# Chunked attention into a Fourier mixing layer: values of the first batch by two queues, column sines late, mirrored halves for the second batch, and instruction orders from fixed lists

## The chip, the cores and the metric

The kernel runs on one core of a Trainium2 chip. The metric is the device time of one execution in microseconds. Engines are named as in the profile: PE (matmul) and its weight loads PEld, DVE (vector), ACT (scalar), POOL (GpSimd) and SP (which here only issues DMAs). DMAs are issued by SP, by ACT and by POOL, each on a queue of its own.

## The reference

Four batches, eight heads, 768 positions, head width 64. The first part is attention in chunks of 32 queries, each of which sees its own chunk, 16 keys to the left, 8 to the right and 8 memory keys:

```
for c in range(nc):
    k_full = concat([mem_k, k[c_start - 16 : c_end + 8]])
    v_full = concat([mem_v, v[c_start - 16 : c_end + 8]])
    a = softmax(q_c @ k_full.T / 8)
    out[c] = a @ v_full
```

The heads are joined to rows x of 768 x 512 per batch, and a mixing layer follows:

```
X = fft(x, axis=1);  X = fft(X, axis=2);  mixed = real(X)
u = x + mixed
un = (u - mean(u)) / sqrt(var(u) + 1e-6)
out = u + relu(un @ w_ch1) @ w_ch2        # 512 -> 2048 -> 512
```

## The kernel before, in words

**Attention.** Work goes by pairs of heads: 16 pairs, n = 0 to 15, four per batch. For a pair, POOL issues the loads of q and k (`e_load_qk`, L375 for the first three batches), SP issues the values (`e_load_v`, seven DMAs: L388 once, L384 four times, L393 twice) into one of four value tiles `va`, PE turns q and k (L403), ACT or DVE copies them out (`e_qT` L421, `e_kT` L446), PE makes scores (L459), ACT the exponentials (L469, L494), PE the values (`e_values`, L511, tiles `xa` and `xo` for the two halves), and DVE normalizes (L521, L522). The value tiles have edges that `e_edges` (L345 to L347) zeroes on DVE or POOL before the load may write.

**Fourier step.** The transform over positions and columns is done by matmuls with cosine and sine tables, which the kernel makes itself at the start: `e_iota` writes index ramps on POOL, DVE turns them to angles (`rS`, `yS` for the rows, `rD`, `yD` in the tile `tri` for the columns), and ACT takes sines (`e_sines`, L1201). `e_negatives` and `e_table_rows` on POOL make the negated tables. The first batch has its own finer-grained path (`first_fourier`: folds, hi and lo parts in half precision, row matmuls at L717, joins at L731), the later ones go through `fourier` (row matmuls L583). Column matmuls come in two forms: `e_columns` (L756, eight matmuls of 256 columns per tile of 128 rows) and, from batch HALVED on, `h_columns` (L777), which uses the mirror symmetry of the column tables and leaves the combination to ACT (`h_copy`, `h_ends`), DVE (`h_mix`, `h_sum`, tile `mix`) and POOL (`h_sum_back`, L817).

**MLP.** Each batch has three thirds j of 256 rows. Layer 1 is `e_ch1` (L894, tile `ph`) with the ReLU on ACT (L903). Layer 2 is either plain (`e_ch2`, L912, added at L919) or, for the thirds in FAST, a scheme of seven products of half-size blocks (`e_prod`, L961) with sums on DVE (`e_s`, L949; results added at L966). A third in FAST takes normalized rows with their scale; the others are scaled at the end by `rstd`. MIXED is the batch in which both forms occur.

**Order.** The kernel does not leave the order to chance. Every piece of work is a task: engine, cost, prerequisites, the buffers that it takes and gives. `Plan.order` plays them through with a model of engine and DMA times and emits the instructions in that order; each engine then runs its own in sequence. Before, tasks have ranks, at each step an engine takes the first by rank that is ready in the model, and a table `moved` overrides about eighty of the ranks. `settled` sets these ranks and calls `order`. Where PE would be idle at the start, filler matmuls on a zero tile (`idle`, L1025 and L1033) stand in the order. `t_gate`, a tiny copy on POOL (L1093) that reads the last value tile of batch 0, keeps POOL's later loads (batch 1 and the weights, `weights`, L1229 and L1234) behind the first batch's values.

Of the kernel before, what the change touches and what calls it, by code (L numbers as in the profile page):

```python
# [10 lines left out]
FP32 = mybir.dt.float32  # L11
# [6 lines left out]
LEFT = 16  # L18
RIGHT = 8
# [18 lines left out]
class Plan:  # L38
# [20 lines left out]
    def add(self, engine, cost, emit, after=(), take=(), give=(), rank=None, moved=0.0,  # L59
            loose=False, late=0.0, filler=False, behind=None, lag=0.0, pick=None, grain=0.1, head=1.0, dense=0.15, mode=""):  # L60
# [3 lines left out]
                 late=late, filler=filler, behind=behind, lag=lag, picks=[pick] if pick else [], grain=grain, head=head, dense=dense, mode=mode)  # L64
        self.tasks.append(t)
        return t

    def share(self, now):
# [4 lines left out]
        while any(left.values()):  # L73
            heads = [xs_[0] + [xs_[0][0]["grain"], q] for q, xs_ in left.items() if xs_]
            live = [h for h in heads if h[2] <= at + 1e-9]
            whole = sum(h[3] for h in live)
            slow = {q: 0.94 if len(live) > 1 and xs_ and xs_[0][0]["grain"] < 0.05 else 1.0
                    for q, xs_ in left.items()}
            step = min([h[1] * whole / h[3] / slow[h[4]] for h in live]
# [5 lines left out]
            for q, xs_ in left.items():  # L85
                if xs_ and xs_[0][2] <= at - step + 1e-9:
                    xs_[0][1] -= step * slow[q] * xs_[0][0]["grain"] / whole
# [14 lines left out]
    def settled(self, moved):  # L102

        for no, rank in moved.items():
            self.tasks[no]["rank"] = rank
        return self.order()

    def order(self):
# [9 lines left out]
        while any(waiting.values()):  # L118
# [5 lines left out]
            for e, ts_ in waiting.items():  # L124
                if idle.get(e, 0.0) > now or (e == "SP" and self.clear > now):
                    continue
                held = False
                for t in ts_:
                    slack = (self.SLACK if e == "PE" and now > self.FIRST and not t["filler"]
                             else 0.0)  # L130
                    if held and not t["loose"]:
                        continue
                    if any(a["done"] is None
                           or (a["end"] > now if a["engine"] == e else a["done"] > now - slack - t["lag"])
                           for a in t["after"]):
                        held = held or (e == "SP" and not t["loose"])
                        continue
# [11 lines left out]
                    if any(self.free[tag] < m for tag, m in need.items()):  # L149
                        held = held or (e == "SP" and not t["loose"])  # L150
                        continue
# [34 lines left out]
            if not moved:  # L186
                recent = [t for t in recent if t["done"] + 8.0 > now] + placed[known:]
# [3 lines left out]
                         + [t["done"] + x for t in recent for x in (0.0, self.SLACK, 4.0, 8.0)  # L191
# [9 lines left out]
def kernel(  # L201
# [15 lines left out]
    P = 128  # L217
# [11 lines left out]
    HALVED = 2  # L229
# [41 lines left out]
    FAST = [(1, 1), (1, 2)] + [(b, j) for b in range(2, B) for j in range(3)]  # L271
    MIXED = 1
# [17 lines left out]
    tri = fpool.tile([P, 3, 2, HD], FP32, tag="hT", bufs=1, name="tri")  # L290
# [87 lines left out]
    def e_load_v(n):  # L378
# [3 lines left out]
        def run(p0, count, t0, nt, key, hh):  # L382
            vb = v[b, 2 * pr + hh]
            nc.sync.dma_start(v1[p0:p0 + count, hh, t0:t0 + nt, 0:D],  # L384
                              bass.AP(tensor=vb.tensor, offset=vb.offset + key * D,
                                      ap=[[D, count], [64 * D, nt], [1, D]]))

        nc.sync.dma_start(v1[OWN:OWN + 64, :, 0, 0:D],  # L388
                          v[b, 2 * pr:2 * pr + 2, 0:64].rearrange("h p d -> p h d"))
# [602 lines left out]
    t_mkf = add("ACT", 1.3, e_mkf, moved=2.04, grain=0.077)  # L992
# [19 lines left out]
    t_kzs = add("ACT", 2.9, e_kzs, [t_table], rank=-2)  # L1012
    for i in range(NV):
# [57 lines left out]
    t_gate, LATE, t_flip = None, 0.3, [None]  # L1071
# [4 lines left out]
    def attention(n):  # L1076
# [5 lines left out]
                      take=(("qs", "ks")[i],), moved=2.02 if b >= TURNED else 1.2, grain=0.089 if b >= TURNED else 0.081,  # L1082
# [3 lines left out]
        lv = add("SP", 2.5, lambda: e_load_v(n), [t_edges[n] if n < NV else None, t_used.get(("va", n % NV))],  # L1086
                 behind=t_x2.get(b - 2),
# [516 lines left out]
```

## Time and profile before

| what | value |
| --- | --- |
| time, median of 3 runs | 274.52 us (274.36 to 275.14) |
| the profiled execution, time | 274.5 us |
| the profiled execution, span | 272.8 us |
| PE busy | 264.2 us, 97% |
| DVE busy | 196.8 us, 72% |
| ACT busy | 160.6 us, 59% |
| POOL busy | 83.3 us, 31% |
| mean DMA rate | 147 GB/s |
| granted PE clock | 1.00 |

The span reaches from the first to the last instruction. Busy times are shares of that span. PE's busy time includes the filler matmuls at the start (11.0 us at L1025 and 7.2 us at L1033, counted as the profile counts them). A wait of an engine is named by what ended it.

### The profile page before, as it was taken

Reading aid. Unit: us, or ns where it says so; the run is one execution under the profiler, and the core shown is the slowest. Engines: PE = TensorE matmul, PEld = TensorE weight load, DVE = VectorE, ACT = ScalarE, POOL = GpSimd, SP = SyncE. Lnnn points to the kernel's source line nnn. Section 1 sums busy time; section 2 is a strip of 40 time slices with the busy share of each in tenths; the row PEclk is TensorE's granted clock in tenths of the full one; section 3 lists DMA queues with packets and bytes.
Section 4 is the critical chain, followed back from the end, with each engine's and each line's share of the span. In section 5 each row is a group of like instructions: output and inputs, shape, how many; then the busy total and the mean of one; then the engine's idle time right before and its main releaser. Section 6 shows DMA issues by size and latency. Waiting matters only on the chain.

```text
span 272.8 us, 8305 instructions
## 1 busy us (share of the span) xinstructions
PE 264.2 (97%) x3449; PEld 216.1 (79%) x3449; DVE 196.8 (72%) x437; ACT 160.6 (59%) x299; POOL 83.3 (31%) x154
## 2 busy tenths in 40 slices
PE   8999897999999999999999989999999999999995
PEld 8667796898766689569678878889899888888884
DVE  8944868940437999699999896879977958444444
ACT  6898568687755579547863738727164381715150
POOL 8991682450111028026237444010100343100000
PEclk9999999999999999999999999999999999999999
DMA  6977999999999899997999995558641038222152
GB/s 115 165 135 141 169 220 211 196 197 198 200 156 241 167 250 225 151 121 193 186 162 220 174 166 138 67 138 190 113 134 21 1 88 166 60 108 48 70 87 77
DMA packets 116118, 40.00 MB, mean 147 GB/s; under 512 B 104560, under 2 KB 111472, under 8 KB 116080
## 3 DMA queue, kind: packets, MB, share of 16 engines
q1 hardware_dynamic: 93888, 23.54, 47.7%
q0 software_dynamic: 21472, 15.21, 34.0%
q10 hardware_dynamic: 720, 0.72, 0.8%
q8 instruction: 27, 0.44, 0.7%
q14 instruction: 11, 0.09, 0.1%
HBM read 37.36 MB, written 13.37 MB: 186 GB/s over the span
## 4 chain that ended last, share of the span: by engine, by line
PE 76%; DVE 11%; SPq 4%; ACT 3%; issue 2%; POOL 2%; DMA 1%; DVEq 0%; POOLq 0%
PE ph L894 29%; PE pc L961 13%; PE pc L912 10%; PE ps L583 5%; PE xa L511 4%; PE xo L511 3%; PE ps L717 3%; SPq L384 2%; PE pm L756 2%; DVE S L949 2%; DVE xsb L966 2%; DVE hT L949 2%; PE sc L482 1%; DMA va<-in_mem_v_dram 1%; PE pm L777 1%
## 5 line engine op out<-in xcount | busy, mean ns | idle before, releaser
L894 PE MATMUL ph<-unT,w_sb 128*128 128x256 f16 x768 | 88.9, 273 | 0.0
L894 PEld LDWEIGHTS <-w_sb 128*128 128x128 f16 x768 | 74.0, 98 | 9.5 <-issue 0.6
L903 ACT ACTIVATE hT<-ph 128x512 f16<-128x512 f32 x96 | 55.9, 598 | 42.1 <-PE pc L961 16.8
L961 PEld LDWEIGHTS <-hT 128*128 128x128 f16 x320 | 31.0, 98 | 5.3 <-issue 1.3
L961 PE MATMUL pc<-w_sb,hT 128*128 128x256 f16 x256 | 32.0, 273 | 0.7 <-DVE xsb L966 0.6
L966 DVE TENSOR_TENSOR xsb<-pc,xsb 128x256 f32<-128x256 f32 x57 | 23.6, 420 | 9.7 <-PE pc L961 8.1
L912 PE MATMUL pc<-w_sb,hT 128*128 128x512 f16 x128 | 29.5, 380 | 0.0
L912 PEld LDWEIGHTS <-hT 128*128 128x128 f16 x128 | 12.1, 98 | 12.9
L949 DVE TENSOR_TENSOR S<-hT 128x768 f16<-128x768 f16 (+1 forms) x16 | 7.9, 491 | 19.2 <-ACT hT L903 18.7
L494 ACT ACTIVATE e<-sc,mbias 96x192 f32<-96x192 f32 (+1 forms) x48 | 18.5, 472 | 3.4 <-PE sc L482 3.4
L469 ACT ACTIVATE e<-sc,mbias 96x384 f32<-96x384 f32 x32 | 16.7, 571 | 3.2 <-PE sc L459 3.1
L817 POOL TENSOR_TENSOR xsb<-mix,xr 128x512 f32<-128x512 f32 x6 | 8.8, 1470 | 30.4 <-ACT mix L811 25.0
L829 DVE BATCH_NORM_STATS2 st<-xsb 128x6 f32<-128x512 f32 x24 | 16.4, 685 | 2.2 <-POOL xsb L817 1.9
L961 PE MATMUL pc<-w_t,S 128*128 128x256 f16 x128 | 15.8, 273 | 0.8 <-DVE xsb L966 0.5
L511 PEld LDWEIGHTS xa<-va,e 96*64 96x64 f32 x384 | 12.6, 138 | 4.5 <-issue 2.7
L511 PE MATMUL xa<-va,e 96*64 96x65 f32 x384 | 14.9, 226 | 1.0 <-DMA va<-in_mem_v_dram 1.0
L595 ACT CAST up<-ps 128x386 f16<-128x386 f32 x12 | 7.3, 606 | 14.2 <-PE ps L583 14.1
L843 ACT ACTIVATE un<-xsb,rs 128x512 f16<-128x512 f32 x16 | 12.4, 807 | 5.0 <-POOL rs L858 5.0
L961 PEld LDWEIGHTS <-S 128*128 128x128 f16 x128 | 12.3, 98 | 2.6 <-issue 0.6
L375 POOL DMA_DIRECT2D qs<-in_q_dram x12 | 8.1, 676 | 20.5 <-PE trq L403 17.8
L511 PE MATMUL xo<-va,e 96*64 96x65 f32 x384 | 14.1, 223 | 0.0
L626 POOL DMA_DIRECT2D xr<-x_back x3 | 2.4, 791 | 35.2 <-DMA x_back<-x_rows 35.2
(191 smaller groups left out, 501.6 us busy)
## 6 DMA issues: line engine op xcount, KB each, us to landing
va<-in_v_dram SPq DMA_DIRECT2D x32, 220.0 KB
w_sb<-in_moe_w_ch_dram POOLq DMA_DIRECT2D x8, 512.0 KB, 16.0
out_dram<-xsb SPq DMA_DIRECT2D x12, 256.0 KB
qs<-in_q_dram POOLq DMA_DIRECT2D x12, 192.0 KB, 5.9
ks<-in_k_dram POOLq DMA_DIRECT2D x12, 192.0 KB, 6.1
x_rows<-xsb POOLq DMA_DIRECT2D x3, 768.0 KB, 4.6
xr<-x_back POOLq DMA_DIRECT2D x3, 768.0 KB, 6.8
out_rows<-xsb SPq DMA_DIRECT2D x9, 256.0 KB
```

Source lines behind the costliest of these rows:

```text
L469: nc.scalar.activation(e1[0:KEYS, :, :, ts(half, 32)], sc[0:KEYS, :, 0:6, ts(half, 32)], AFT.Exp, bias=mbias[0:KEYS, half:half + 1], scale ...
L494: nc.scalar.activation(to, src, AFT.Exp, bias=mbias[0:KEYS, half:half + 1], scale=1.0 / math.sqrt(D))
L511: nc.tensor.matmul(xa[64 * half:64 * half + 64, st, hh, 0:65], e1[0:KEYS, hh, t6, :], v1[0:KEYS, hh, 6 * g + t6, 0:65], start=True, stop=True)
L583: nc.tensor.matmul(out_[:, sp, :], part[:, ab, sp * 3 + st, c0:c1], tab[:, sp, st, :], start=(st == 0 and i == 0), stop=(st == 2 and i == 1))
L829: nc.vector.bn_stats(st6, xs[b][:, kt, :])
L843: nc.scalar.activation(un, xs[b][:, kt, :], AFT.Identity, bias=rs[:, 1:2], scale=rs[:, 0:1])
L894: nc.tensor.matmul(ph[:, k, :], w1_sb[:, dt, ts(HH * k + i, P)], unT_of[b, j][:, dt, :], start=(dt == 0), stop=(dt == NDT - 1))
L903: nc.scalar.activation(hT_of[b, j][:, :, i, :], ph, AFT.Relu, bias=0.0, scale=1.0 if (b, j) in FAST else -1.0)
L912: nc.tensor.matmul(pc_of[b, j, r], hT_of[b, j][:, k, i, ts(r, P)], w2_sb[:, HH * k + i, :], start=(i + k == 0), stop=(i + k == HH))
L949: nc.vector.tensor_tensor(out_[:, lo:hi], a[:, lo:hi], c[:, lo:hi], op)
L961: nc.tensor.matmul(pc_of[key], a[:, i, :], w[:, i, :], start=(i == 0 and new), stop=(i == HH - 1), skip_group_check=not new)
L966: nc.vector.tensor_tensor(u, pc, u, ALU.add)
```

## The change

**Values of batch 0.** `e_load_v` takes a half: for the first four pairs SP issues six of the seven DMAs, and the large one of the second head is issued by ACT as a task of its own (`t_lb`). The order of the two queues is set so that the DMAs that share a completion semaphore lie apart. The edge memsets and the loads of q and k stand in a new order on POOL.

**Column sines late.** The four row sines are taken first, then ACT loads the table of exponentials. The column sine and cosine come after the last exponential of batch 0, with a second load of the sine table and another of the exponential table. `tri`, which holds their angles, moves to the buffer `w2t`. The row tables' negatives wait for the row sines alone; `e_table_rows` waits for the late ones.

**Batch 1 by halves.** HALVED is 1 instead of 2, FAST holds all thirds of batches 1 to 3, MIXED is 0: batch 1 goes through `h_columns` and its companions, and its first third goes through the seven products.

**Lists.** `moved` is replaced by one list of task numbers for each engine, and `order` takes the head of each list and nothing else. The DMA model has a cap per transfer (`rates`). One copy of k (`e_kT`, pair 2) goes to DVE. The seven products wait each for the weight sum that it uses instead of for all.

```diff
-    HALVED = 2
+    HALVED = 1
...
-    FAST = [(1, 1), (1, 2)] + [(b, j) for b in range(2, B) for j in range(3)]
-    MIXED = 1
+    FAST = [(b, j) for b in range(1, B) for j in range(3)]
+    MIXED = 0
...
-    tri = fpool.tile([P, 3, 2, HD], FP32, tag="hT", bufs=1, name="tri")
+    tri = wpool.tile([P, 3, 2, HD], FP32, tag="w2t", bufs=1, name="tri")
...
-    def e_load_v(n):
+    def e_load_v(n, half=None):
...
+        if half == 1:
+            run(OWN - LEFT, LEFT + 64, 1, NT - 1, 64 - LEFT, 1, nc.scalar)
+            return
         nc.sync.dma_start(v1[OWN:OWN + 64, :, 0, 0:D],
                           v[b, 2 * pr:2 * pr + 2, 0:64].rearrange("h p d -> p h d"))
         for hh in range(2):
-            run(OWN - LEFT, LEFT + 64, 1, NT - 1, 64 - LEFT, hh)
-            run(OWN + 64, RIGHT, 0, NT - 1, 64, hh)
+            if half is None or hh == 0:
+                run(OWN - LEFT, LEFT + 64, 1, NT - 1, 64 - LEFT, hh, nc.sync)
+            run(OWN + 64, RIGHT, 0, NT - 1, 64, hh, nc.sync)
...
+        if first:
+            if n % 2 == 0:
+                for m in (n, n + 1):
+                    t_lb[m] = add("ACT", 0.6, lambda m=m: e_load_v(m, 1), [t_edges[m]], moved=0.9, grain=0.038,
+                                  head=2.2, late=LATE, cap=0.67, rank=-4 + 0.1 * m,
+                                  behind=t_lb[m - 1] if m % 2 else t_lv.get(m - 1))
+            lb = t_lb[n]
...
-            t_gate = add("POOL", 0.1, e_gate, [lv])
+            t_gate = add("POOL", 0.1, e_gate, [lv, lb])
...
-            dve = ("DVE", nc.vector.tensor_copy) if n < 2 else ("ACT", None)
+            dve = ("DVE", nc.vector.tensor_copy) if n < 3 else ("ACT", None)
...
-    for what, par in ((0, 0), (0, 1), (1, 0), (1, 1), (2, 0), (3, 0)):
...
+    for what, par in ((0, 0), (0, 1), (1, 0), (1, 1)):
+        t_sines = sine(what, par, [t_sines], 0.78 if what < 2 else 0.72)
+    t_warm = add("ACT", 1.6, lambda: nc.scalar.activation(warm, zero, AFT.Exp), [t_sines], rank=SINES)
...
+    for what in (2, 3):
+        t_late = sine(what, 0, [t_exp[n, g] for n in range(HP) for g in range(2)] if what == 2 else [t_late],
+                      2.0 if what == 2 else 0.72)
+        t_late["rank"] = LATER
+    t_warm = add("ACT", 1.6, lambda: nc.scalar.activation(warm, zero, AFT.Exp), [t_late], rank=LATER)
     t_neg = shared(add("POOL", 3.3, e_negatives, [t_sines], rank=100))
-    t_rows = shared(add("POOL", 2.8, e_table_rows, [t_sines, t_neg], rank=101))
+    t_rows = shared(add("POOL", 2.8, e_table_rows, [t_late, t_neg], rank=LATER))
...
-                     e_prod(b, j, m, lo, hi, bank_), after + mlp_prev + t_sums[:3] + [c2],
+                     e_prod(b, j, m, lo, hi, bank_), after + mlp_prev + {6: t_sums[1:2], 5: t_sums[:1], 7: t_sums[2:3]}.get(m, []) + [c2],
...
-                for t in ts_:
...
+                for t in ts_[:1]:
...
-    moved = {
-        0: 392.49, 8: 192.95, 9: 752.99, 11: 739.23, 18: 736.64, 31: 392.15, 32: 196.77, 36: 174.88,
...
+    lists = {
+        "DVE": [
+            16, 7, 0, 4, 22, 20, 21, 23, 5, 24, 26, 25, 27, 33, 35, 41, 45, 28, 29, 57, 61, 75, 79, 49, 53, 65,
...
+        "PE": [
+            17, 42, 34, 44, 46, 60, 58, 50, 48, 78, 62, 52, 66, 64, 76, 68, 80, 93, 84, 95, 82, 86, 97, 125,
+            101, 99, 127, 103, 126, 128, 213, 145, 146, 147, 148, 211, 151, 230, 215, 133, 169, 170, 228, 176,
...
+        "ACT": [
+            3, 1, 38, 6, 43, 105, 72, 106, 107, 39, 108, 109, 47, 73, 59, 51, 63, 67, 77, 81, 94, 85, 117, 118,
+            96, 121, 122, 98, 102, 110, 130, 131, 149, 136, 139, 140, 143, 210, 111, 150, 214, 153, 156, 212,
...
+        "POOL": [
+            36, 2, 11, 37, 55, 54, 13, 15, 18, 71, 9, 8, 19, 12, 70, 113, 10, 14, 88, 89, 32, 91, 208, 207,
+            225, 224, 244, 243, 135, 124, 245, 246, 114, 242, 241, 265, 264, 354, 260, 353, 205, 368, 261, 367,
...
+        "SP": [
+            40, 56, 74, 90, 209, 247, 226, 266, 355, 369, 397, 280, 383, 500, 487, 488, 485, 654, 328, 330,
...
```

Some of the numbers: on POOL 36, 37, 54, 55, 70, 71, 88, 89 are the loads of q and k of pairs 0 to 3, 2 the iota, 11, 13 and 9 the edges of value tiles 2, 3 and 1, 15 the masks, 113 the negatives, 114 `e_table_rows`, 91 the gate, 241 to 244 the first-layer weights. On ACT 38, 39, 72, 73 are the value DMAs of pairs 0 to 3, 105 to 108 the row sines, 47, 51, 63, 67, 81, 85, 98, 102 the exponentials, 110 and 111 the column sine and cosine. On PE 97 and 101 are the scores and 99 and 103 the values of pair 3, 125 to 128 and 145 to 148 the row matmuls of the two halves, 617 the first MLP matmuls.

More of the change, by code (lines that the diff above doesn't have):

```diff
@@ L75, in share @@
             live = [h for h in heads if h[2] <= at + 1e-9]
[L76 to L79, printed above, removed]
+            rate = self.rates(live)
+            step = min([h[1] / rate[h[4]] for h in live]
                        + [h[2] - at for h in heads if h[2] > at + 1e-9])
@@ L86, in share @@
                 if xs_ and xs_[0][2] <= at - step + 1e-9:
-                    xs_[0][1] -= step * slow[q] * xs_[0][0]["grain"] / whole
+                    xs_[0][1] -= step * rate[q]
             if had > self.ROOM >= load():
@@ L126, in order @@
                     continue
-                held = False
-                for t in ts_:
[L129 to L132, printed above, removed]
+                for t in ts_[:1]:
                     if any(a["done"] is None
-                           or (a["end"] > now if a["engine"] == e else a["done"] > now - slack - t["lag"])
-                           for a in t["after"]):
-                        held = held or (e == "SP" and not t["loose"])
+                           or (a["end"] if a["engine"] == e else a["done"]) > now + 1e-9 for a in t["after"]):
                         continue
@@ L186, in order @@
             if not moved:
-                recent = [t for t in recent if t["done"] + 8.0 > now] + placed[known:]
+                recent = [t for t in recent if t["done"] > now] + placed[known:]
                 known = len(placed)
```

79 lines of the change are left out of this document (55 added, 24 removed), and 59 rows, old and new, of tables (lists, moved).

## The prediction

> **What bounds the kernel now.** I read the page first, then the busy time by stage, then the chain of waits, and last the first 52 us engine by engine.
>
> ```profile
> span 272.8 us, 8305 instructions
> ```
> ```profile
> 31.60:52.00 20.40, 18.60 (x277) 16.47 (x276) 16.89 (x38) 13.54 (x26) 10.65 (x20) 1.00 1.13 205
> 52.00:90.00 38.00, 38.00 (x601) 28.53 (x592) 17.84 (x41) 25.44 (x44) 8.55 (x16) 1.00 1.13 199
> 90.00:160.00 70.00, 69.22 (x935) 53.97 (x934) 65.32 (x129) 46.09 (x90) 27.56 (x35) 1.00 1.24 184
> 160.00:269.60 109.60, 108.86 (x1114) 96.06 (x1113) 75.07 (x176) 50.83 (x100) 14.35 (x26) 1.00 0.43 96
> ```
>
> The columns behind a stretch are its length, then busy PE, PE weight loads, DVE, ACT and POOL, the granted clock, the DMA share and GB/s. From 52 us to 269.6 us PE is idle for 1.5 us in all, at full clock. So the end moves by two things only: when that dense stretch begins, and how much PE work lies in it. The span is 272.8 us and the same execution's time is 274.5 us, so 1.7 us lie around it; the median of the runs is 274.52 us, and I sum against 274.5.
>
> What sets the beginning is in the chain that ended last, and in the SP queue.
>
> ```profile
> 26.66 3.33 DMA va<-in_mem_v_dram
> 30.12 0.80 PE xa L511 x20
> 31.62 6.16 PE ps L717 x72
> 38.26 1.13 PE ps L717 x12
> 39.41 0.57 DVE join L731
> 52.12 2.73 PE ph L894 x24
> ```
> ```profile
> 4.30 0.31 SPq L393 DMA_DIRECT2D va<-in_mem_v_dram  x1
> 14.64 0.62 SPq L388 DMA_DIRECT2D va<-in_v_dram  x1
> ```
> ```profile
> 0.91 0.57 POOL L326 IOTA tri<- 128x512 f32 x1 [0.40 <-POOLq L1588]
> 1.89 0.89 POOL L375 DMA_DIRECT2D qs<-in_q_dram  x1
> 2.78 1.49 POOL L1072 MEMSET kU<- 128x800 bf16 x2
> 8.42 0.18 POOL L345 MEMSET va<- 128x24 f32 x1
> 8.90 0.63 POOL L375 DMA_DIRECT2D qs<-in_q_dram  x1
> 14.37 0.14 POOL L345 MEMSET va<- 128x24 f32 x1
> 29.16 0.79 POOL L1093 COPY gate<-va 1x1 f32<-1x1 f32 x1 [7.41 <-DMA va<-in_v_dram]
> 34.72 2.21 POOL L1229 DMA_DIRECT2D w_sb<-in_moe_w_ch_dram  x4
> 42.62 0.74 POOL L1234 DMA_DIRECT2D w_sb<-in_moe_w_ch_dram  x1 [2.46 <-DMA w_sb<-in_moe_w_ch_dram]
> 50.61 0.77 POOL L1234 DMA_DIRECT2D w_sb<-in_moe_w_ch_dram  x1 [1.76 <-DMA w_sb<-in_moe_w_ch_dram]
> ```
>
> SP issues the values of pair 0 until 4.6 us and then nothing until 14.64, where the edge memsets of the next value tile have been written (the POOL memset at 14.37). From there it issues three pairs; the last lands about 3.33 us after 26.66, and PE starts the last pair's values at 30.12. The rows of the first Fourier step follow from 31.62 without a gap to 39.4, joins, columns and norms fill the time to 52.12, and there the MLP starts. The gate on POOL, which holds back every load of batch 1 and of the weights, opens at 29.16 for the same reason. Counting POOL's DMAs from the gate, the last weight load at 50.61 is the eighth after the last of the four first-layer chunks issued at 34.72, as the one at 42.62 is the eighth after the first. I read both waits as the landing of those chunks: 42.6 and 50.6, 2.7 us per chunk. So the MLP's start at 52.12 has only 1.5 us over its weights.
>
> **The change, part by part.** *Values earlier.* In the new POOL list the edges of tile 1 come behind q0, the iota, two other edge sets, k0, k1, q1, the masks, one kTb memset and k2. The memset row at 8.42 stands behind the same work except that it has the kU memsets (1.49) in place of the two edge sets, which take 0.48 each (8.42 to 8.90). So tile 1 is ready near 8.42 - 1.49 + 2 x 0.48 + 0.48 = 8.4. Against 14.64 that is 6.2 us earlier. At the old issue rate, giving the second queue nothing, the last values would land at 30.0 - 6.2 = 23.8 and the gate would open there. The shares of the DMA engines say there is room:
>
> ```profile
> 5.00:14.00 9.00, 9.00 (x126) 6.16 (x124) 8.24 (x15) 7.53 (x10) 8.38 (x23) 1.00 1.13 174
> 14.00:30.00 16.00, 15.07 (x343) 9.75 (x335) 8.55 (x18) 14.34 (x27) 8.08 (x22) 1.00 0.76 143
> ```
>
> Some (1.13 - 0.76) x 16 / 1.13 = 5.2 us of transfer time lie unused between 14 and 30 us.
>
> *What is late next.* The exponentials on ACT:
>
> ```profile
> 0.80 1.30 ACTq L361 DMA_DIRECT2D mkf<-in_mem_k_dram  x2
> 11.22 0.63 ACT L1201 ACTIVATE sinD<-tri 128x512 f16<-128x512 f32 x1 [0.18 <-DVE tri L1057]
> 12.80 1.28 ACT L1218 ACT_TABLE_LOAD   x1
> 14.24 1.04 ACT L469 ACTIVATE e<-sc,mbias 96x384 f32<-96x384 f32 x2
> 28.04 1.04 ACT L469 ACTIVATE e<-sc,mbias 96x384 f32<-96x384 f32 x2
> ```
>
> The iota, from which the angles come, now stands behind the first q issue (0.89 us later), and ACT gets three value issues of about 0.65 us ahead of its first exponential or just behind it (a fourth comes early, where ACT still waits for the angles); two column sines (0.63 and about as much) leave. These cancel within half a microsecond, so the exponentials begin near 14.3 as before and the last ends near 29.2 (29.08 now): one kTb copy leaves ACT for DVE, one cast comes ahead of them. Values of the last group then end at about 30.2 instead of 31.6, and two of the seven remaining row groups (84 matmuls in 7.29 us, so 24 in 2.1) are already done, because the new PE list puts them between the last values. That makes the joins 1.4 + 2.1 = 3.5 us earlier at best. Against it: q3 and k3 now stand behind the negated tables on POOL, and the late sines cost ACT two further table loads of 1.28 right behind the last exponential. I take 1 us for these: 2.5 us earlier.
>
> *Weights.* Two first-layer chunks are issued before, two behind the column tables (t_rows), which wait for the late cosine. By my walk along ACT's list (29.2, load 1.28, sine 0.63, some 3.2 us of casts, cosine 0.7) the cosine is ready near 35, POOL's tables near 38, and the last chunk is issued at 39 instead of 36.9. But its queue starts 5 to 6 us sooner with the gate: landing near 48.4 to 50.4 by the old pace of 2.7 us a chunk. That allows an MLP start of 49.6, so the 2.5 us stand.
>
> The Trainium skill, "ScalarE: Activation LUTs", section "What ACT_TABLE_LOAD costs", speaks against the late sines: it counts about 2.66 us for a switch of set, with a drain, and advises doing all of one set at once. The row shows 1.28 and the next activation directly behind it; by the page's figure the cosine, and with it the last weight chunk, would come some 1.4 us later still.
>
> *PE work that goes.* Batch 1 takes the mirrored columns, and third (1,0) the seven-product second layer.
>
> ```profile
> 50.97 0.87 PE pm L756 x8
> 72.36 3.45 PE pc L912 x16
> 148.33 0.55 PE pm L777 x8
> 165.34 0.87 PE pc L961 x8
> ```
>
> Three column tiles save 3 x (0.87 - 0.55) = 0.96. The third goes from 2 x 3.45 = 6.9 to 7 x 0.87 = 6.1, saving 0.8. Together 1.75 us, all of it in the dense stretch, so it counts whole.
>
> *DVE work that comes.*
>
> ```profile
> 0.00:272.80 272.80, 25.40 (x56) 1.00 0.83 147
> 0.00:272.80 272.80, 23.60 (x57) 1.00 0.83 147
> 0.00:272.80 272.80, 10.30 (x30) 4.24 (x22) 8.82 (x6) 1.00 0.83 147
> L919 DVE SCALAR_TENSOR_TENSOR xsb<-pc,rstd,xsb 128x512 f32<-128x512 f32 x8 | 6.0, 744 | 7.2 <-PE pc L912 7.1
> L821 DVE TENSOR_TENSOR xsb<-pm,xsb 128x512 f32<-128x512 f32 x9 | 6.0, 672 | 1.9 <-PE pm L756 1.9
> ```
>
> The first two rows are DVE's time at the seven-product sums (L949) and at the adds of its results (L966), each for eight thirds; the third is the mix tile, for two batches. The third (1,0) costs (25.4 + 23.6) / 8 - 2 x 0.744 = 4.6 us more; the halves 10.3 / 2 less six sums of about 0.67, some 1.1 more. That is 5.7 us on an engine with 4.7 us free from 90 to 160 us, but 20 us free from 52 to 90, into which batch 1 moves with its earlier loads. PE is idle for 0.78 us between 90 and 160, where it waits for DVE; the cost of the new work lies between nothing (earlier inputs cover it) and 5.7 - 4.7 = 1.0; I take 0.4, nearer the idle now seen. The halves' POOL sums (8.82 / 2) and ACT copies (4.24 / 2) fall where those engines are idle a third of the time and more; without that cover they would add their 4.4 and 2.1 us to a batch that PE does not need for several microseconds.
>
> *The lists.* Fixed lists change the order, not the work. Before, too, each engine ran a fixed sequence. I cost them at nothing beyond the above; what they could still win is PE's idle of 1.8 us between 31.6 and 52.
>
> Sum: 274.5 - 2.5 - 1.75 + 0.4 = 270.7 us.
>
> **The rivals.** *The startup gives nothing.* Moving values into 5 to 14 us, where the DMA share is already 1.13, may only push q and k back; then the last scores, not the values, are as late as the last values were. Against it stands the 0.76 behind. PE's saving alone would give 274.5 - 1.75 = 272.8. The Trainium skill, "DMA: Bandwidth & Descriptors", section "Issuing engines are not separate DMA queues", supports this rival: DMAs started on several engines run on the same 16 DMA engines, and a second starter saves only the time of starting. Here that start, not the transfer, is what stood idle.
>
> *Slower: the weights late.*
>
> ```profile
> DMA to landing us min/median/max: 7.6/16.0/20.3
> ```
>
> This row is the weight chunks'. If the last first-layer chunk, issued at 39, takes the median 16.0 us, it lands at 55.0, where the MLP started at 52.1 before: 2.9 us late, less PE's 1.75, so 1.2 us slower, 275.7; at 20.3 it would be 280.0. It decides from a landing 14.8 us after issue. For it: four q and k loads and two chunks still stand ahead in the queue. Against it: the last chunk of before took 50.6 - 36.9 = 13.7 with three chunks ahead of it.
>
> *Slower: ACT held by its own queue.* A value DMA on ACT that must wait for an older DMA holds every exponential behind it. Two waits of a landing (3.33 each) would give 270.7 + 6.7 = 277.4; it decides from 3.8 us of such waits. The SP issue rows show waits of this kind, but the new order spaces the ACT issues apart.
>
> *Better.* The 3.5 us in full, and the 1.8 us of idle gone: 274.5 - 3.5 - 1.75 - 1.8 = 267.5.
>
> **How the numbers follow.** What a measurement of this kernel can tell from no change is about 0.3%, 0.8 us. My forecast, 269 to 272, has 0.55; better 0.06; startup without gain 0.13; these are faster, 0.74. Late weights have 0.15 and a held ACT 0.07: slower, 0.22; in between 0.04. The range runs from the better case, 267.5, to just over late weights at the median, 276.0.
>
> **What would show it.** SP's second pair issued near 8.4 us, and the gate's copy near 24. The last exponential near 29, the joins near 37, the first MLP matmul near 49.6, PE idle under 2 us from there on, 96 matmuls on L912 and 504 on L961's lines instead of 128 and 448. Right in direction but wrong in step would be an MLP start at 52 with a shorter dense stretch. Wrong altogether: PE idle ahead of ph with a weight DMA as its releaser, or ACT waiting at a va DMA.

## The result, and the profile after

| | before | changed |
| --- | --- | --- |
| time, median | 274.44 us (4 runs, 274.24 to 275.14) | 271.06 us (4 runs, 270.31 to 278.94) |
| ratio of the undisturbed runs | | 0.9869, 95% interval 0.9825 to 0.9913 |
| the profiled execution: time, span | 274.5, 272.8 | 270.31, 268.6 |
| PE busy, idle within the span | 264.2, 8.6 | 262.2, 6.4 |

The medians count every execution; the ratios leave out those more than 1.5% above the fastest of the same kernel, here the one of 278.94 us (granted clock 0.988). The kernel is faster by 1.3%, 3.6 us of 274.4; the profiled executions differ by 4.2 us.

The first two lines are from the page of the changed kernel, the others its busy time by stage (length, then busy PE, PEld, DVE, ACT, POOL, granted clock, DMA share, GB/s):

```profile
span 268.6 us, 8357 instructions
...
PE 262.2 (98%) x3469; PEld 216.9 (81%) x3469; DVE 203.0 (76%) x456; ACT 161.9 (60%) x312; POOL 89.6 (33%) x159
```
```profile
14.60:31.60 17.00, 17.00 (x353) 11.30 (x353) 11.66 (x23) 11.40 (x22) 9.72 (x23) 1.00 1.18 196
31.60:52.00 20.40, 19.86 (x355) 17.09 (x351) 17.03 (x38) 17.80 (x33) 8.77 (x20) 1.00 1.17 205
52.00:90.00 38.00, 38.00 (x611) 28.89 (x606) 23.78 (x49) 27.26 (x47) 9.59 (x17) 1.00 1.13 192
90.00:160.00 70.00, 69.45 (x978) 56.68 (x978) 65.58 (x149) 47.38 (x108) 34.14 (x45) 1.00 1.16 179
160.00:265.50 105.50, 105.42 (x1034) 93.65 (x1030) 73.31 (x168) 47.36 (x90) 15.01 (x22) 1.00 0.43 94
```

and the two stages of the kernel before that were not shown yet:

```profile
14.60:31.60 17.00, 15.95 (x377) 11.06 (x377) 9.16 (x20) 13.75 (x25) 9.20 (x20) 1.00 0.75 146
160.00:265.50 105.50, 104.77 (x1080) 92.80 (x1080) 72.20 (x170) 50.83 (x100) 14.35 (x26) 1.00 0.44 98
```

Idle PE between 14.6 and 52 us went from 2.85 to 0.54 us, from 52 to 265.5 us from 1.51 to 0.63. The DMA share of 0.75 in the second stage is now 1.18. It is not the first batch's values that fill this time: for the most part they moved ahead of it. POOL's loads of the second batch and of the weights do, which go out sooner because the gate opens sooner. POOL's queue from 14.6 to 31.6 us, before and changed (packets, MB, share of the 16 engines; packets overlap, so shares can add up to more than 1):

```profile
q0 software_dynamic: 206, 0.19, 8.0%
```
```profile
q0 software_dynamic: 1609, 2.09, 73.4%
```

SP's queue went from 66.1% to 30.6% there, and ACT's new one has 12.9%.

But a PE that is never idle is not a PE that is further on, as the moments show that answer to the prediction's rows (the timeline by engine; in brackets the idle time before, with its releaser):

```profile
7.89 0.63 SPq L399 DMA_DIRECT2D va<-in_v_dram  x1
...
19.59 0.18 POOL L1119 COPY gate<-va 1x1 f32<-1x1 f32 x1
...
31.07 1.04 ACT L481 ACTIVATE e<-sc,mbias 96x384 f32<-96x384 f32 x2 [0.78 <-PE sc L471]
32.13 1.28 ACT L1228 ACT_TABLE_LOAD   x1
33.42 0.63 ACT L1228 ACTIVATE sinD<-tri 128x512 f16<-128x512 f32 x1
...
39.61 0.56 DVE L743 TENSOR_TENSOR join<-top,ps 128x386 f32<-128x386 f32 x1 [1.80 <-PE ps L729]
...
53.49 4.53 PE L906 MATMUL ph<-unT,w_sb 128*128 128x256 f16 x40
```

SP issues the second pair at 7.89 instead of 14.64, the gate opens at 19.59 instead of 29.16. Yet the last exponentials end at 32.11 (29.08 before), the joins begin at 39.61 (39.41), the MLP at 53.49 (52.05). The chain that ended last says what lies between (start, length, what):

```profile
14.06 1.83 PE idle L1038 x8
...
27.94 0.97 PE idle L1038 x4
...
36.44 3.15 PE ps L729 x36
```

It runs along PE's own sequence, and the filler matmuls (`idle`: dummy products put where PE would else stand idle) are links of it. Between 14.6 and 31.6 us they take 7.55 us of PE in place of 5.74, though their number over the whole kernel fell from 118 to 114. So PE's own sequence bounds this stretch, where the DMAs did before; the experiment with half the fillers tests that. The MLP starts 1.44 us later, the joins only 0.2: second-batch attention now stands ahead of the MLP, and its value products take 0.85 and 0.70 us on the chain there. The first rows are the changed kernel's second-batch value products, the last two those of the kernel before:

```profile
49.85 0.92 PE L523 MATMUL xa<-va,e 96*64 96x65 f32 x24
...
58.23 0.92 PE L523 MATMUL xa<-va,e 96*64 96x65 f32 x24
```
```profile
56.75 0.92 PE L511 MATMUL xa<-va,e 96*64 96x65 f32 x24
...
68.56 0.92 PE L511 MATMUL xa<-va,e 96*64 96x65 f32 x24
```

They come 6.9 and 10.3 us earlier. This matters below.

### The profile page after: what moved, and what is told of

Read it like the earlier page. It is cut to its first block, busy times and chain, and to the rows that moved or that the text cites. A ratio compares the mean times of both kernels' runs of the same rounds, so it can differ in the third digit from the quotient of the medians.

```text
span 268.6 us, 8357 instructions
## 1 busy us (share of the span) xinstructions
PE 262.2 (98%) x3469; PEld 216.9 (81%) x3469; DVE 203.0 (76%) x456; ACT 161.9 (60%) x312; POOL 89.6 (33%) x159
## 4 chain that ended last, share of the span: by engine, by line
PE 82%; DVE 13%; POOL 2%; issue 2%; ACT 0%; POOLq 0%
PE ph L906 27%; PE pc L973 21%; PE pc L924 5%; PE ps L595 5%; PE xa L523 4%; PE xo L523 4%; PE idle L1038 3%; PE ps L729 3%; PE pm L768 2%; PE sc L471 2%; PE trk L415 2%; DVE st L841 1%; DVE xsb L534 1%; PE pm L789 1%; PE trq L415 1%
## 5 line engine op out<-in xcount | busy, mean ns | idle before, releaser
L973 PE MATMUL pc<-w_sb,hT 128*128 128x256 f16 x288 | 36.6, 273 | 0.0
L978 DVE TENSOR_TENSOR xsb<-pc,xsb 128x256 f32<-128x256 f32 x64 | 26.1, 420 | 13.8 <-PE pc L973 12.8
L829 POOL TENSOR_TENSOR xsb<-mix,xr 128x512 f32<-128x512 f32 x9 | 12.4, 1389 | 45.1 <-ACT mix L823 35.5
L924 PE MATMUL pc<-w_sb,hT 128*128 128x512 f16 x96 | 21.7, 379 | 0.0
L855 ACT ACTIVATE un<-xsb,rs 128x512 f16<-128x512 f32 x18 | 14.4, 820 | 5.3 <-POOL rs L870 5.3
L973 PE MATMUL pc<-w_t,S 128*128 128x256 f16 x144 | 17.4, 273 | 0.0
L973 PEld LDWEIGHTS <-S 128*128 128x128 f16 x144 | 14.0, 98 | 1.6
L523 PEld LDWEIGHTS xa<-va,e 96*64 96x64 f32 x384 | 12.5, 137 | 2.3 <-issue 1.7
L1038 PE MATMUL idle<-dz 128*128 128x512 bf16 x46 | 12.9, 387 | 1.0 <-DVE va L353 1.0
L433 ACT COPY qT<-trq 128x768 bf16<-128x768 bf16 x12 | 9.5, 795 | 6.6 <-PE trq L415 6.4
L523 PEld LDWEIGHTS xo<-va,e 96*64 96x64 f32 x384 | 12.6, 138 | 0.4 <-ACT e L481 0.2
```

The lines of the kernel that those rows point to most:

```text
L523: nc.tensor.matmul(xa[64 * half:64 * half + 64, st, hh, 0:65], e1[0:KEYS, hh, t6, :], v1[0:KEYS, hh, 6 * g + t6, 0:65], start=True, stop=True)
L855: nc.scalar.activation(un, xs[b][:, kt, :], AFT.Identity, bias=rs[:, 1:2], scale=rs[:, 0:1])
L924: nc.tensor.matmul(pc_of[b, j, r], hT_of[b, j][:, k, i, ts(r, P)], w2_sb[:, HH * k + i, :], start=(i + k == 0), stop=(i + k == HH))
L973: nc.tensor.matmul(pc_of[key], a[:, i, :], w[:, i, :], start=(i == 0 and new), stop=(i == HH - 1), skip_group_check=not new)
L978: nc.vector.tensor_tensor(u, pc, u, ALU.add)
L1038: nc.tensor.matmul(fill_of[0], dz, strided(dz, 0, [[0, 4], [1, P]]), start=True, stop=True)
```

## The experiments

Each time is set against runs of the kernel before on the same chip, whose medians were 274.34 to 274.81 us. All but one, the one in the old order, start from the changed kernel.

**One queue.** Does the second queue give anything?

```diff
-            run(OWN - LEFT, LEFT + 64, 1, NT - 1, 64 - LEFT, 1, nc.scalar)
+            run(OWN - LEFT, LEFT + 64, 1, NT - 1, 64 - LEFT, 1, nc.sync)
```

> The large value DMA of the second head goes back to SP's queue for the first four pairs; everything else, the lists included, is the changed kernel's. Theory A (in the changed kernel the start is set by PE's own sequence of fillers, scores and values, since the gate already opens at 19.6 us and the last values come at 32.9): SP's last value issue and the gate come up to 3 us later, about 22, and the time stays within 0.5 us of 270.3. Theory B (the second queue is what the gain rests on): the gate goes back towards 24 or later and the time rises by 2 us or more.

Measured: median 275.55 us (5 runs, 270.32 to 277.45). The profiled execution took 270.32 us against the changed kernel's 270.31, with joins at 39.62 against 39.61 and the gate at 19.59 in both; ratio to before 0.9886 (0.981 to 0.9962), which rests on the two lowest runs. By the profiled executions the second queue is worth nothing that shows. That three of five runs took 275.55 us or more, against one of four of the changed kernel, has no profile and stays open. The Trainium skill, "DMA: Bandwidth & Descriptors", section "Issuing engines are not separate DMA queues", says that a second starter saves only the time of starting; by that rule, the trace agrees.

**No fillers after 12 us.**

```diff
+            if t["emit"] in (plan.fill, plan.fine) and t["at"] > 12.0:
+                continue
```

> The filler matmuls planned after 12 us are left out (they compute nothing that is used); all else is the changed kernel. Theory A (fillers placed by the plan hold the scores back, ACT waits 6.5 us for scores in the first 60 us): the last exponential ends 2 to 4 us earlier than 32.1, the joins 2 us earlier than 39.6, the time falls by 1 to 2.5 us, to 268 to 269.3. Theory B (the start is bound by loads of q and k of pair 3 or by the weights): no change within 0.5 us. Theory C (the fillers keep the granted clock up): the clock falls below 0.95 somewhere before 50 us and the time rises by 1 us or more.

Measured: median 278.77 us, ratio 1.0111 (1.0035 to 1.0187). The stages of its profiled execution (279.95 us):

```profile
14.60:31.60 17.00, 13.09 (x308) 11.79 (x307) 12.11 (x25) 11.50 (x22) 9.17 (x21) 0.80 1.14 178
31.60:52.00 20.40, 14.58 (x203) 12.77 (x203) 9.81 (x22) 11.21 (x22) 8.25 (x21) 0.83 1.07 195
```

The granted clock falls to 0.80 and 0.83. The fillers hold the clock, as theory C has it. Not all of the drop need come of their absence alone: PE also waits 5.48 us in one piece for the first batch's last values here, with 0.50 behind it. And all or none is too coarse a test of whether they also hold the work.

**Half the fillers.**

```diff
+            if t["emit"] in (plan.fill, plan.fine) and t["at"] > 12.0:
+                late += 1
+                if late % 2:
+                    continue
```

> The changed kernel with every second group of filler products (products that nothing reads, lines L1038 and L1046) that was planned after 12 us left out; all else as in the changed kernel, 270.3 us. Its chain of waits from 14.6 to 31.6 us is PE's own sequence with fillers in it, 15.6% of the first 60 us. Theory C (the fillers only stand where PE would wait anyway, and hold the clock): the granted clock stays near 1.0, the joins stay at 39.6 and the time at 270.0 to 270.6. Theory F (with the values by two queues the data are there earlier, and the fillers themselves now hold PE's sequence): joins near 38, time 268.5 to 269.5. Theory G (half of them is too few for the clock): granted clock under 0.9 from 14.6 to 52 us and 272 to 276 us, on the way to the 0.80 and 278 us without any.

Measured: median 277.17 us (271.21 to 278.19). The profiled execution (275.65 us), by stage, then a narrow stretch, then two moments:

```profile
14.60:31.60 17.00, 16.29 (x380) 12.41 (x379) 13.43 (x28) 13.81 (x25) 11.31 (x26) 1.00 1.19 197
31.60:52.00 20.40, 19.84 (x341) 17.04 (x338) 17.02 (x38) 17.66 (x32) 8.12 (x21) 1.00 1.15 204
...
61.50:66.00 4.50, 4.46 (x90) 4.28 (x91) 0.75 (x2) 0.00 (x0) 0.20 (x1) 0.50 0.84 141
```
```profile
37.12 0.56 DVE L743 TENSOR_TENSOR join<-top,ps 128x386 f32<-128x386 f32 x1 [1.84 <-PE ps L729]
...
61.54 0.77 PE L523 MATMUL xa<-va,e 96*64 96x65 f32 x9 [3.23 <-DMA va<-in_mem_v_dram]
```

Up to 52 us theory F is right: the clock stays at 1.00, the last exponential ends at 29.58 instead of 32.11, the joins come at 37.12, 2.5 us earlier, and the MLP at 51.13 instead of 53.49. Fillers take 3.96 us between 14.6 and 31.6 us in place of 7.55. So the full set of fillers does hold PE back. Then PE waits 5.3 us in two pieces for the second batch's second pair of values, the clock drops to 0.50 behind that, and all is lost. Both sides of this wait moved: PE asks for the values at 55.94 us, 2.3 us sooner than the changed kernel, and their last transfer goes out at 53.98, 2.2 us later. Theory F's time is refuted: even the lowest of the six, 271.21, is above the changed kernel's usual 270.3 to 271.

**The gate later.** It reads an element of the fourth pair that the large transfer of its second head brings, which lands early; here it reads one of SP's last.

```diff
-                nc.gpsimd.tensor_copy(gate[64:65], va[n % NV][64:65, 1, NT - 1, 0:1])
+                nc.gpsimd.tensor_copy(gate[0:1], va[n % NV][0:1, 1, NT - 1, 0:1])
```

> The changed kernel with the gate of the second batch's loads reading an element that SP's own last transfer of the fourth pair writes, in place of one of ScalarE's transfer; the gate then opens when all values of the first batch have landed, near 24 us and not at 19.6. Theory H (the early gate lets the weights and the second batch's loads into the last 5 us of the values, and makes these late): the last values end 1 us earlier or more (31.0 to 32.9 in place of 33.84), joins 38.5, time 269.3 to 269.9. Theory I (PE's own sequence sets the joins, the values are there in time): values and joins unmoved, time 270.0 to 270.6. Theory J (the weights follow the gate and become the late ones): first ph product at 55 or later in place of 53.5, time 271 to 273.

Measured: median 279.12 us (271.48 to 280.91); joins at 39.62, first ph product at 53.49, so none of H and J; nor I, since the time is worse. Its timeline on POOL and on SP (an issue's length is the time for which it holds SP):

```profile
26.97 0.18 POOL L1119 COPY gate<-va 1x1 f32<-1x1 f32 x1 [7.43 <-DMA va<-in_mem_v_dram]
...
30.41 11.55 SPq L392 DMA_DIRECT2D va<-in_v_dram  x2
...
57.77 0.32 SPq L405 DMA_DIRECT2D va<-in_mem_v_dram  x1
```

POOL's weights now go out at 29.97, and two of SP's issues stand for 11.55 us. The second pair's last transfer is issued at 57.77, and PE waits for it until 64.82. In the changed kernel it goes out 6.0 us sooner:

```profile
51.77 0.31 SPq L405 DMA_DIRECT2D va<-in_mem_v_dram  x1
```

By the semaphores of its trace it has landed at 57.98 us, 0.25 us before PE asks at 58.23. So the changed kernel has hardly any margin here. (The expectation of *The changed kernel again*, below, takes 39.8 us for this issue and gets a margin of 11 us. The issue that ends at 39.8 belongs to the third pair, whose values stand ahead of the second's in SP's list.)

SP's issues stand longest behind POOL's weight transfers in three kernels: weights at 34.72 and an issue of 5.99 us from 38.26 before, 22.63 and 6.44 from 25.42 in the changed kernel, 29.97 and 11.55 from 30.41 here. That POOL's loads crowd out SP's is read from this order. The queues of the changed kernel from 25 to 34 us, behind its first two weight transfers (packets, MB, share of the 16 engines), fit it:

```profile
q0 software_dynamic: 783, 1.51, 90.2%
q1 hardware_dynamic: 1399, 0.35, 22.5%
```

q0 is POOL's, q1 SP's: 1.9 KB a packet against 0.25 KB. The Trainium skill, "DMA: Bandwidth & Descriptors", section "Queues, rings and completion order", says that each DMA engine goes round its queues packet by packet. No run shows that turn itself, but by it the large packets take most of the time, and the shares are in line with that. They don't test it, since POOL's queue also moved more bytes.

**Halves undone.** Batch 1's columns and its third (1,0) as before, the changed kernel's start, lists and order otherwise.

```diff
-    HALVED = 1
+    HALVED = 2
...
-        if (b, j) not in FAST:
+        if (b, j) not in FAST or (b, j) == (1, 0):
```

> Batch 1 takes the full column matmuls and its first third the plain second layer again (the rows stay normalized ahead, as in the changed kernel); order, queues and sines are the changed kernel's, with the old tasks in the places of the new ones. The prediction's step (PE work counts whole): PE work rises by 1.75 us and the time by 1.5 to 2.6 us, to 271.8 to 272.9. The rival (DVE, not PE, is the limit in 90 to 160 us, and the halves with their 5.7 us of DVE work cost as much as they bring): the time rises by less than 0.8 us or falls.

Measured: median 274.94 us (11 runs, 273.79 to 282.85), ratio to before 1.0022 (0.9976 to 1.0068), the profiled execution 273.79 us. It does the same as the changed kernel to the MLP's start (joins 39.61, ph 53.49) and differs behind it:

```profile
90.00:160.00 70.00, 68.01 (x881) 51.80 (x880) 57.63 (x121) 42.91 (x89) 29.83 (x41) 1.00 1.21 174
160.00:265.50 105.50, 105.50 (x1074) 93.93 (x1072) 73.67 (x172) 50.63 (x99) 15.57 (x22) 1.00 0.44 98
```
```profile
PE pm L768 <- DVE xsb L655: 1.4, 1, 1.4
```

This is the cleanest split of the change. By the profiled executions, of 4.2 us 3.5 are batch 1's halves and products, and the start with everything in it is worth what is left, 0.7. By the ratios the halves are worth about 4.2 us and the start -0.6 (-1.9 to 0.7), which can't be told from nothing. The 3.5 are PE work and waits: from 52 us to 265.5, PE's idle time is 1.99 us here and 0.63 in the changed kernel (1.36), the rest, 2.1 us, is work. All of that difference in waits is the one of the last line, and it arises in an order that was not made for batch 1's old form.

**Sines early.** The column sines stand ahead of the first exponential again, without the second pair of table loads.

```diff
-        t_late = sine(what, 0, [t_exp[n, g] for n in range(HP) for g in range(2)] if what == 2 else [t_late],
-                      2.0 if what == 2 else 0.72)
+        t_late = sine(what, 0, [t_sines] if what == 2 else [t_late],
+                      0.72)
```

> The column sine and cosine are taken before the first exponential again (their angles earlier on DVE too), so the second pair of table loads goes; the rest of the lists stays. If the late sines are what the gain at the start rests on: the first exponential comes about 1.4 us later than 13.3 and the time rises by about 1 us. If PE's sequence with its fillers sets the start (theory A): the fillers planned around the first scores absorb most of the 1.4 us and the time stays within 0.5 us. If the two table loads (2 x 1.28 us) on ACT cost as much as they bring: faster by up to 1 us.

Measured: median 271.73 us (11 runs, 271.70 to 274.30), ratio 0.9911 (0.9884 to 0.9938). The late sines are worth 0.7 us by the medians and 1.4 by the lowest times (271.70 against 270.31); the intervals overlap, so this is not shown. The profile fell on the slowest of the eleven, so where it would come from isn't shown either. It is also the most even kernel of all: nine of eleven executions lie within 0.3 us.

**Halves in the old order.** The kernel before with batch 1 as changed (HALVED 1, all of batches 1 to 3 in FAST); the old steps keep their order, the new ones stand where those stood that they replace.

```diff
-    HALVED = 2
+    HALVED = 1
...
-    MIXED = 1
+    MIXED = 0
```

> The kernel before (274.4 us) with batch 1's columns by mirrored halves and all three of its second layers by the seven products, in the old order of the engines: the old steps in the order that they had, the new ones at the places of those that they replace. Values, sines and the gate as before. Theory A (whatever PE is spared in batch 1 is saved whole): first-layer and second-layer products and columns 2.55 us less on PE, so 271.5 to 272.3. Theory K (the longer way from the columns' halves over the adds to the next first layer needs the new order): PE waits for the adds between 90 and 160 us, where the busy share falls under 67.5 of 70, and the time is 273.5 or more, up to 276.

Measured: 282.59 us median, ratio 1.0295 (1.0251 to 1.034). Its stage and its longest wait on PE (in all, times, longest):

```profile
90.00:160.00 70.00, 64.10 (x884) 50.26 (x883) 63.08 (x126) 42.64 (x89) 24.70 (x34) 0.93 1.11 173
```
```profile
PE ph L894 <- DMA unT<-un: 3.8, 1, 3.8
```

Theory K, and more than it expected: PE idles 5.9 us in this stage, at a clock of 0.93. The chain behind the longest wait runs over DVE's adds and statistics and ends with the transposing DMA of `un`, which the line names. Two microseconds less work are worth nothing without an order for the new, longer way. This shows my order to be bad, not that none near the old one would do.

**The changed kernel again.**

> The changed kernel itself, timed again beside the runs below. Its first profile asks for the second batch's second pair of values at 58.23 us, and SP had issued that pair's last transfer by 39.8 us; in the kernels with half the fillers and with the late gate, where weight transfers from GpSimd's queue came between, the same issue was done at 47.9 and 57.8 us and TensorE stood 5.3 and 6.2 us for it, with the clock at 0.91 between 52 and 90 us after that. Theory L (the changed kernel stands near the same edge, since it asks for these values 10.3 us earlier than the kernel before, which asks at 68.56): executions of two kinds, some at 270.3 to 271, others at 275 to 279 with a clock under 0.99, and none between. Theory M (its margin of 11 us over the landing is enough): all at 270.3 to 272.

Measured: median 270.91 us (270.49 to 279.75, 6 runs), ratio 0.9869 (0.983 to 0.9908). Between 271.77 and 279.75 there is nothing; theory L's two kinds are there, the second rare. In this kernel's profile the second pair's last transfer lands 1.3 us before PE asks for it, in the changed kernel's 0.25 us: an edge it does stand near. But no profile shows one of the rare executions, so that it is the same wait stays a guess.

**Keeping the lead: four kernels.** All move POOL's weight transfers. The first three (with half the fillers, with all, with a third: `late % 3`): the second pair of first-layer transfers behind q and k of the eighth pair, the first second-layer one behind k of the tenth.

```diff
-            ... 245, 246, 114, 242, 241, 265, 264, 354, 260, 353, 205, 368, 261, 367,
+            ... 245, 246, 114, 265, 264, 242, 241, 354, 353, 205, 368, 260, 261, 367,
```

> Half of the fillers after 12 us, and on GpSimd's queue the second pair of first-layer weight transfers moved behind the loads of q and k of the eighth pair, the first second-layer transfer behind the k of the tenth pair. Theory L (GpSimd's transfers push the second batch's values out): no wait for values near 58 us, granted clock 1.0 to the end, the lead of 2.5 us that half the fillers gave is kept: 268.0 to 269.5, in most executions. Theory N (the weights become the late ones): the first ph product waits for w_sb, 271 or more.

> The same moves on GpSimd's queue, with all of the changed kernel's fillers. Theory L: 270.2 to 270.8 in most executions, with fewer of 275 and more than the changed kernel has beside it. Theory N: first ph product later than 53.5 us, 271 to 274.

> As with half the fillers and the later weights, but only a third of the fillers after 12 us kept. Theory G (the clock needs them): granted clock under 0.95 between 14.6 and 52 us and 272 or more. Otherwise PE comes 1 us further ahead: 267.5 to 269.

Measured: with half the fillers median 278.28 us (271.31 to 279.55); with all 277.54 (271.59 to 280.06), ratio 0.993 (0.989 to 0.997); with a third 275.09 (268.90 to 280.59), ratio 0.9854 (0.981 to 0.9899). The profiles of the first two are of executions of 279.55 and 271.62 us. The third's ratio rests on four of its twelve executions. One row of each in this order:

```profile
36.49 1.35 PE L523 MATMUL xa<-va,e 96*64 96x65 f32 x20 [3.82 <-DMA va<-in_mem_v_dram]
```
```profile
57.42 1.91 PE L906 MATMUL ph<-unT,w_sb 128*128 128x256 f16 x16 [1.14 <-DVE xsb L534]
```
```profile
17.99 0.29 PE L471 MATMUL sc<-qT,kTb 64*128 64x64 bf16 x8 [1.29 <-issue]
```

The wait near 58 us is gone in all three, as theory L says, but another appears: one for the first batch's last values (POOL's queue had 100% of the engines from 25 to 34 us and SP's 11.5%), one for DVE, and one of 1.29 us without a releaser, behind which the clock of the kernel with a third is 0.64 between 14.6 and 31.6 us. DVE's wait stands in a low execution, so it doesn't explain the median of 277.54: seven of those twelve took over 277 us with every filler in place. What makes them slow is open. The kernel with a third also had the two lowest executions of all, 268.90 and 269.35 us. They have no profile; that in them nothing was late is likely, not shown.

*Half the fillers, weights after the values*: the first pair of weight transfers to about 30 us too.

```diff
-            225, 224, 244, 243, 135, 124, 245, 246, 114, 242, 241, 265, ...
+            225, 224, 135, 124, 244, 243, 245, 246, 242, 241, 114, 265, ...
```

> Half of the fillers after 12 us, as before, the first pair of weight transfers on GpSimd's queue moved from behind the loads of q and k of the sixth pair (issued at 22.6 us) to behind the middle column's sums (near 30 us), and the second pair directly behind the next q and k, ahead of the table rows. Theory L (weights that overtake the values on the 16 engines make the values late: the queue of GpSimd took 90% and SP's 20% of them from 25 to 34 us): SP's values for the second batch are issued as in the kernel before, done by 31 us for the first of its pairs, no wait of PE for values, granted clock 1.0, 267.8 to 269.5 in most executions. Theory O (the executions near 275 to 280 come of having fewer fillers, whatever the order of loads): most of them at 275 to 280 again, with waits of under 1 us for values. Theory N (weights late): PE waits for w_sb before the first ph product at 51 us, 270 to 273.

Measured: median 277.15 us (272.82 to 279.95), ratio 1.0089 (1.0053 to 1.0126). PE waits 0.4 us for values in place of 5.3, but now a load of q is late:

```profile
23.60 0.53 PE L415 MATMUL trq<-ident_b,qs 96*64 96x96 bf16 x16 [1.77 <-DMA qs<-in_q_dram]
```
```profile
26.00:30.00 4.00, 4.00 (x66) 3.04 (x62) 2.75 (x6) 2.75 (x5) 0.23 (x1) 0.50 0.93 166
```

Theory L is not borne out as a cure. Nine of the ten executions took over 275 us, as theory O forecast; but the kernel with all fillers and the moved weights was slow as well, so too few fillers can't be the whole cause. The profile, with its 0.4 us for values, is of the lowest execution; none of the slow ones has one. The DMA share is 1.06 and more from 14.6 us to 52; whether some order of the loads leaves nothing late is open. No version beats the changed kernel's median.

## Why the prediction was right, and where its steps were not

The time, 270.7 forecast, came out at 271.06 (profiled: 270.31), inside 269 to 272, faster. Its sum was 2.5 for the start, 1.75 for PE work, less 0.4. The parts measured otherwise.

*The start, 2.5 us: mis-sized, 0.7 by the profiled executions, nothing by the ratios.* "Values earlier" held: the second pair at 7.89 (8.4 forecast). The gate, near 24 by my reading, opened at 19.59, with no wait at all: POOL came to it right behind its own memsets, and the element it reads, from a transfer issued at 13.30, was there. It does so too where SP issues that transfer (one queue). The step that failed is *What is late next*: I named the exponentials and let them begin and end as before. They begin earlier, at 13.29, but end at 32.11 and not at 29.2, since ACT waits 5.6 us for scores between 12.5 and 33 us (0.8 before, 3.3 with half the fillers), and these stand in a PE sequence with 7.55 us of fillers in the second stage in place of 5.74. Joins at 37 and the MLP at 49.6 did not come. With half the fillers the last exponential ended at 29.58, the joins came at 37.12 and the MLP at 51.13, so the 2.5 us at the joins lay there, but the second batch's values were not there in time to keep them.

*PE work, 1.75 us: right as to size.* 96 and 504 matmuls on the two second-layer lines, as forecast. The groups of the changed kernel and of the kernel with batch 1 as before:

```profile
L973 PE MATMUL pc<-w_sb,hT 128*128 128x256 f16 x288 | 36.6, 273 | 0.0
L924 PE MATMUL pc<-w_sb,hT 128*128 128x512 f16 x96 | 21.7, 379 | 0.0
L973 PE MATMUL pc<-w_t,S 128*128 128x256 f16 x144 | 17.4, 273 | 0.0
L973 PE MATMUL pc<-w_t,hT 128*128 128x256 f16 x72 | 9.3, 272 | 0.0
```
```profile
L973 PE MATMUL pc<-w_sb,hT 128*128 128x256 f16 x256 | 32.4, 273 | 0.0
L924 PE MATMUL pc<-w_sb,hT 128*128 128x512 f16 x128 | 29.3, 379 | 0.0
L973 PE MATMUL pc<-w_t,S 128*128 128x256 f16 x128 | 15.4, 273 | 0.0
L973 PE MATMUL pc<-w_t,hT 128*128 128x256 f16 x64 | 8.3, 272 | 0.0
```

The second layer takes 85.0 against 85.4 us, 0.4 less where I had 0.8; the columns' groups, added up the same way, 20.3 against 21.2, 0.9 where I had 0.96. That is 1.3 by the groups and 2.1 by the stages, and 1.75 lies between.

*DVE's leak, 0.4 us more: wrong sign.* DVE's adds fill 65.58 of 70 us between 90 and 160, but PE waits there for 0.55 us, against 0.78 before, and idle time from 52 us on fell by 0.9. I costed the lists at nothing beyond the start; together with the earlier inputs they paid for the longer way of the halves, which in the old order cost 5.9 us of idle PE.

The startup without gain, a rival at 0.13, was nearer on the start than the forecast; its 272.8 lacked the idle time that went. Late weights did not come: no wait for a weight transfer shows, and the weight chunks took 9.3 us from issue to landing at the median in place of 16.0. ACT was not held by its queue: its value issues took 0.65 us and three times 0.32. The table loads took 1.28 us with the sine 1.31 behind the last exponential's end; the drain that the Trainium skill, "ScalarE: Activation LUTs", section "What ACT_TABLE_LOAD costs", adds to a switch is not seen there. So the mechanism was right for PE's work in batch 1 and wrong for the start, and the time was right by luck, by two errors that cancelled: 1.8 us too much for the start, and behind it, by the profiled executions, 3.5 us in place of 1.75 - 0.4 = 1.35, 2.1 too little.

## What to carry to other kernels

A faster supply is worth what the next engine in line leaves of it: look at the consumer's own sequence, its fillers too, before counting the saved wait. A change that spares an engine work needs the order made anew with it, and gains twice when that order also takes out waits. Where loads share the engines and run full, moving one earlier can make another late; look at the margin between landing and use of each, and time such a kernel often.

## What the runs showed that I had not expected

A short stall can cost more than itself. The kernel with halves in the old order waits 1.57 us for the first batch's last values, and behind that the clock is 0.50. The kernel before waits 1.59 us for an exponential, and the clock stays at 1.00. For each, the row of the wait and a stretch behind it, the old order first:

```profile
30.55 0.94 PE L511 MATMUL xa<-va,e 96*64 96x65 f32 x20 [1.57 <-DMA va<-in_mem_v_dram]
```
```profile
32.00:34.00 2.00, 2.00 (x24) 1.79 (x21) 2.00 (x4) 0.46 (x2) 1.86 (x4) 0.50 1.00 155
```
```profile
44.33 0.35 PE L459 MATMUL sc<-qT,kTb 64*128 64x64 bf16 x12 [1.59 <-ACT e L469]
```
```profile
44.00:50.00 6.00, 5.46 (x77) 4.39 (x77) 5.26 (x13) 4.68 (x9) 1.28 (x2) 1.00 1.07 204
```

Waits of 1.29 and 1.77 us (above) were followed by 0.50 as well, and so was one of 1.27 without the late fillers; one of 1.41 with batch 1 as before and one of 1.74 with half the fillers and the weights later were followed by 1.00. So the length of one wait does not decide it, and what does is not shown. The Trainium skill, "TensorE: Matmul & The Clock Gate", section "HAM oscillation — how this bites in real kernels", warns of idle gaps over about 3.4 us; here the drop came behind waits of 1.27 to 1.77 us in four places. Where nearly every microsecond is PE's, a wait of 1.3 to 1.8 us is a risk, though not a certain loss.
